# Sliding-window attention and a mixture of experts on one core: sums moved behind the next minimum, one pool of PSUM banks, four stages for seven

## Chip, core and metric

One core of a Trainium2 chip runs the whole kernel. The metric is device time in microseconds, the median of several runs; a profiled execution gives the trace. Engines are called PE (TensorE), DVE (VectorE), ACT (ScalarE), POOL (GpSimd) and SP (the queue that issues most transfers). Names such as L684 are lines of the kernel.

## What is computed

```python
# attention: 8 sequences x 8 heads, 576 positions, head size 64, float32
scores = 1/sqrt(64) * q @ k.T            # heads 0-3: the last 32 positions
                                         # heads 4-7: every 4th of the last 128
attn = softmax(masked scores); x = attn @ v      # x: (4608, 512)
# mixture of 8 experts, each token to one
logits = x @ w_gate; e = argmax(logits); g = softmax(logits)[e]
out = g * (relu(x @ w1[e]) @ w2[e])      # w1: 512 x 1024, w2: 1024 x 512
```

## The kernel before

**Attention.** A sequence has eight units: two types (ty 0 near window, ty 1 every fourth position), two pairs of heads (hl), two halves (g). `front` (L260) makes a unit's scores in PSUM (L270), scales and masks them into `e` on DVE (L282), takes the minimum of each block, `lo` (L292), runs six or eight exponentials on ACT (L295) that leave their sums in `den`, adds 1e-9 (L303) and takes the reciprocal (L305) on DVE, and multiplies on POOL (L306). `weights` (L311) transposes the result on PE (L317) and copies it out as `eT`. `summed` (L324) multiplies by v (L337) and copies out `xT`. `turn` (L216) transposes q and k for the next pair of heads. `attention` (L353) writes, in step i: front of unit i, weights of unit i−2, in every second step the two turns, and summed of unit i−2 (LAG is 2). The copies out of PSUM go by `evac` (L175) to DVE and ACT in turn, so they carry lines 178 and 180.

**Routing.** When a sequence has ended, `route` (L389) transposes its rows (L396), computes logits (L407), the expert of each token and its rank among the tokens of that expert (a DVE chain and two matmuls, L449 and L456), and scatters the rows into a bucket for each expert by six indirect transfers on POOL's queue (L156).

**Experts.** 43 slots of up to 128 tokens of one expert, each 32 matmuls into `ph` (L684), relu, 8 into `py` (L708; each float32 matmul is two records), and a scatter of the result (L717). Which expert a slot has is known only on the chip: `tables` (L494) computes it for a stage of slots in some 25 small DVE operations. A stage's slots are those that must be full after so many sequences. SP loads the tables' values and then the tokens and, if the expert differs from that of the slot two before, 2 MB of w1 and 2 MB of w2 into one of two buffers.

**Order.** All engines issue in written order. The text interleaves three generators: attention, routing and the slots. Each piece has a cost (a scores step 1.2, weights 0.8, a turn 0.7, summed 0.9, a slot's pieces 0.93, 0.88 and 0.5, 14.98 in all). After each attention piece the slots are owed its cost times a rate; a stage's slots may run 14 after its tables were written, and the rate is then what is left, over 42. What is left over when attention and routing have ended runs alone.

**PSUM.** Two tiles of two banks (scores, weights, turned), one bank (xo, routing), two for ph, one for xt and py.

Of the kernel before, what the change touches and what calls it, by code (L numbers as in the profile page):

```python
# [45 lines left out]
def _constants():  # L46
# [23 lines left out]
    }  # L70


    for s, (_, j0, j1) in enumerate(STAGES):
        place = np.append((np.arange(E) - 3 * s) % E, E)
        parts[f"upto{s}"] = np.tile((place[None] <= place[:, None]).reshape(1, -1), (128, 1))
# [15 lines left out]
def kernel(  # L91
# [14 lines left out]
    ctx.enter_context(tc.manual_schedule())  # L106
# [60 lines left out]
    def bank2(name):  # L167
        return big.tile([128, 2, 512], F32, tag="big", name=name)

    def bank(name):  # L170
        return one.tile([128, 512], F32, tag="one", name=name)

    flip = [0]

    def evac(dst, src):  # L175
        flip[0] ^= 1
        if flip[0]:
            nc.vector.tensor_copy(dst, src)  # L178
        else:
            nc.scalar.copy(dst, src)  # L180
# [35 lines left out]
    def turn(b, ty, hl, name):  # L216

        src = t[b, name, ty]  # L220
        dst = pool.tile([128, S], F32, tag=name + "T", name=name + "T", bufs=2)
        ps = bank2("turned")
        if ty == 0:
            for i in range(NT):
                nc.tensor.transpose(  # L225
                    ps[:, i // 3, TT * (i % 3) : TT * (i % 3) + TT],
                    src[:, i, 2 * hl : 2 * hl + 2, :].rearrange("p h d -> p (h d)"),
                    ident[0:TT, 0:TT],
                )
            evac(dst.rearrange("p (a t) -> p a t", a=2), ps[:, :, 0:288])  # L230
        else:
            for h in range(2):
                for m in range(4):
                    nc.tensor.transpose(  # L234
                        ps[:, h, 72 * m : 72 * m + 72],
                        src[:, 2 * hl + h, 128 * m : 128 * m + 128],
                        ident[0:72, 0:72],
                    )
                evac(
                    dst.rearrange("p (h m t a) -> p h a m t", h=2, m=2, a=2)[:, h],  # L240
                    ps[:, h, 0:288].rearrange("p (a m t) -> p a m t", a=2, m=2),
                )
        return dst
# [16 lines left out]
    def front(qT, kT, ty, g):  # L260
# [4 lines left out]
        sc = bank2("scores")  # L265
        for n in range(nb):
            for r in range(2):
                q0, k0, _, _ = bl[r][n]
                rows = slice(DH * r, DH * r + DH)
                nc.tensor.matmul(  # L270
                    sc[0:nq, r, 128 * n : 128 * n + 128],
                    lhsT=qT[rows, q0 : q0 + nq],
                    rhs=kT[rows, k0 : k0 + 128],
                    start=True,
                    stop=True,
                )
# [5 lines left out]
        nc.vector.scalar_tensor_tensor(  # L282
            out=e,
            in0=sc[0:nq, :, 0:w],
            scalar=-SCALE,
            in1=m.unsqueeze(1).broadcast_to([nq, 2, w]),
            op0=OP.mult,
            op1=OP.add,
        )
        ev = e.rearrange("p r (n m) -> p (r n) m", m=128)  # L290
        lo = pool.tile([nq, 2 * nb], F32, tag=f"lo{ty}", name="lo")
        nc.vector.tensor_reduce(out=lo, in_=ev, axis=AX, op=OP.min)  # L292
        den = pool.tile([nq, 2 * nb], F32, tag=f"den{ty}", name="den")
        for n in range(2 * nb):
            nc.scalar.activation(  # L295
                out=ev[:, n],
                in_=ev[:, n],
                func=AF.Exp,
                bias=lo[:, n : n + 1],
                scale=-1.0,  # L300
                accum_out=den[:, n : n + 1],
            )
        nc.vector.tensor_scalar(den, den, 1e-9, None, op0=OP.add)  # L303
        rec = pool.tile([nq, 2 * nb], F32, tag=f"rec{ty}", name="rec")
# [4 lines left out]
        return ev  # L309

    def weights(ev, ty, g):  # L311

        nq, nb = (96, 72)[ty], len(blocks(ty, g)[0])
        tp = bank2("weights")
        for r in range(2):
            for n in range(nb):
                nc.tensor.transpose(  # L317
                    tp[:, r, nq * n : nq * n + nq], ev[:, nb * r + n], ident[0:nq, 0:nq]
                )
        eT = pool.tile([128, 2, 288], F32, tag="eT", name="eT")  # L320
        evac(eT, tp[:, :, 0:288])
        return eT

    def summed(eT, b, xT, ty, hl, g):  # L324
# [20 lines left out]
        if ty == 0:  # L345
            evac(dst, xo[:, 0:288])
        else:
            evac(
# [4 lines left out]
    def attention():  # L353
# [8 lines left out]
        xTs, evs = {}, {}  # L362
        for i in range(len(units) + LAG):
            if i < len(units):
                b, ty, hl, g = units[i]
                evs[i] = front(qT["q"], qT["k"], ty, g)
                yield 1.2, None
            if i >= LAG:
                eT = weights(evs.pop(i - LAG), *[units[i - LAG][n] for n in (1, 3)])
                yield 0.8, None  # L370
# [8 lines left out]
            if i >= LAG:  # L379
# [7 lines left out]
                yield 0.9, (b2, xTs.pop(b2)) if last else None  # L387

    def route(b, xT, bank):  # L389


        rows = []
        for i in range(NT):
# [6 lines left out]
            evac(row[:, 0:DM], ps[0:TT])  # L400
# [85 lines left out]
        for s, (b2, _, _) in enumerate(STAGES):  # L486
            if b2 == b:
                yield
                tables(s, bank)
# [4 lines left out]
    def tables(s, bank):  # L494
# [24 lines left out]
        if last:  # L519
# [18 lines left out]

        ends, end, begin = table("ends", E1, E1), table("end", E1), table("begin", E1)
# [3 lines left out]
            in1=const(f"upto{s}", 1).rearrange("p (a b) -> p a b", b=E1),  # L543
# [114 lines left out]
    def moe():  # L658


        def across(j):
            ps = psy.tile([128, 4, 128], F32, tag="y", name="xt")
# [8 lines left out]
        for j in range(NSLOT):  # L671
# [7 lines left out]
            for fg in range(2):  # L679
                ph = psh.tile([128, 4, 128], F32, tag="h", name="ph")  # L680
# [25 lines left out]
            py = psy.tile([128, 512], F32, tag="y", name="py")  # L706
# [36 lines left out]
    clock = {"moe": 0.0, "all": 0.0, "owed": 0.0, "rate": 0.0, "ready": []}  # L743
    SLOT = 0.5 + 8 * 0.93 + 8 * 0.88

    def run_slots(limit):

        while clock["owed"] > 0:
            now = [r for r in clock["ready"] if r[0] <= clock["all"]]
            upto = max([r[1] for r in now], default=0)  # L750
            if clock["moe"] >= SLOT * upto - 0.01 or clock["moe"] >= limit:
# [7 lines left out]
    def run_routing():  # L759
# [4 lines left out]
        try:  # L764
# [5 lines left out]
            for b2, _, j1 in STAGES:  # L770
                if b2 == b:
                    clock["ready"].append((clock["all"] + 14.0, j1))
                    left = SLOT * j1 - clock["moe"]
                    clock["rate"] = left / 42.0

    for cost, ended in attention():
        clock["all"] += cost
        clock["owed"] += cost * clock["rate"] / 2
        run_slots(1e9)
        if ended:  # L780
            use = bank if ended[0] > 1 else lambda name: psh.tile(
                [128, 512], F32, tag="h", name=name
            )
            routing.append((ended[0], route(*ended, use)))
        run_routing()
        clock["owed"] += cost * clock["rate"] / 2
        run_slots(1e9)
    while routing:
        clock["owed"] = 2.0
        run_slots(1e9)  # L790
# [33 lines left out]
```

## Time and profile before

| | |
|---|---|
| median of 3 runs | 1243.12 us (1242.3 to 1249.36) |
| profiled execution | 1253.76 us, span 1251.5 us |
| PE busy | 998.9 us, 80% of the span; mean granted clock 0.859 |
| DVE, ACT, POOL busy | 376.2 (30%), 305.5 (24%), 202.9 us (16%) |
| transfers | 193 MB, mean 154 GB/s |
| chain that ended last | PE 64%, DVE 15%, ACT 14%, issue 6% |

The shares are means over stretches that differ: attention alone at first, attention with slots, slots alone at the end. A view by stretch (busy time of each engine in windows) and the chain of waits (what released each step of the work that ended last) tell more than the shares. [...]

### The profile page before, as it was taken

The page shows a single profiled execution, that of the slowest core. Times are in us where ns is not written, and L with a number is a line of the kernel's source. Part 1 is how long each engine was busy: PE and PEld are TensorE (multiplying, and loading weights), DVE is VectorE, ACT ScalarE, POOL GpSimd, SP SyncE. Part 2 cuts the span into 40 slices and gives each one's busy share as a digit, 9 for nine tenths or more (in the row PEclk, how much of TensorE's full clock was granted, in tenths as well). Part 3 has the DMA queues.
Part 4 walks back from the last instruction along what each step waited for, and adds up shares of the span by engine and source line. Part 5 has one row for each costly group of instructions (what it writes and reads, how often), then busy time and mean ns, then how long its engine had stood idle before and what let it go on. Part 6 is the DMA issues. An engine that isn't in the chain of part 4 may idle for free.

```text
span 1251.5 us, 18337 instructions
## 1 busy us (share of the span) xinstructions
PE 998.9 (80%) x6922; PEld 762.0 (61%) x6922; DVE 376.2 (30%) x973; ACT 305.5 (24%) x1127; POOL 202.9 (16%) x167
## 2 busy tenths in 40 slices
PE   3546656546768896998789699977979999999996
PEld 2445545445646674666567477755757777777774
DVE  2333333433343334334333533353140110000110
ACT  3333233133123312333233233313100100010100
POOL 1111211211121112112121311122040000000000
PEclk8566556567689968999889999989988999999999
DMA  9022122292066725784338565654567281817910
GB/s 224 1 64 73 38 63 72 76 311 72 6 207 211 250 109 181 229 279 133 82 119 271 182 193 184 202 182 152 170 211 245 103 291 50 286 34 249 320 50 1
DMA packets 137639, 193.23 MB, mean 154 GB/s; under 512 B 68110, under 2 KB 76302, under 8 KB 137424
## 3 DMA queue, kind: packets, MB, share of 16 engines
q1 hardware_dynamic: 129728, 170.98, 42.9%
q0 software_dynamic: 7152, 19.71, 4.5%
q10 hardware_dynamic: 672, 1.37, 0.4%
q8 instruction: 55, 0.90, 0.3%
q14 instruction: 32, 0.26, 0.1%
HBM read 226.60 MB, written 23.11 MB: 200 GB/s over the span
## 4 chain that ended last, share of the span: by engine, by line
PE 64%; DVE 15%; ACT 14%; issue 6%; SPq 1%; DMA 0%; ACTq 0%; POOLq 0%; DVEq 0%
PE ph L684 21%; PE py L708 21%; ACT e L295 12%; PE scores L270 6%; PE xo L337 6%; DVE e L282 5%; DVE lo L292 5%; PE logits L407 4%; PE turned L234 2%; PE xrow L396 2%; PE xt L664 1%; PE turned L225 1%; DVE eT L178 1%; ACT qT L180 1%; ACT kT L180 1%
## 5 line engine op out<-in xcount | busy, mean ns | idle before, releaser
L684 PE MATMUL ph<-xt,w 128*128 128x128 f32 x2752 | 354.0, 284 | 14.5 <-issue 9.5
L684 PEld LDWEIGHTS ph<-xt,w 128*128 128x128 f32 x2752 | 335.8, 198 | 35.4 <-issue 27.4
L708 PE MATMUL py<-w,h 128*128 128x512 f32 x688 | 335.6, 622 | 2.3 <-ACT qT L180 1.8
L295 ACT ACTIVATE e<-e,lo 72x128 f32<-72x128 f32 (+1 forms) x448 | 174.4, 391 | 280.6 <-DVE lo L292 271.5
L306 POOL TENSOR_TENSOR e<-e,rec 96x768 f32<-96x768 f32 (+1 forms) x64 | 107.7, 1683 | 590.0 <-DVE rec L305 292.0
L708 PEld LDWEIGHTS py<-w,h 128*128 128x128 f32 x688 | 124.6, 196 | 115.5 <-issue 109.2
L337 PE MATMUL xo<-eT,v 128*64 128x72 f32 (+1 forms) x896 | 75.2, 297 | 125.4 <-DVE eT L178 60.5
L337 PEld LDWEIGHTS xo<-eT,v 128*64 128x64 f32 x896 | 61.9, 179 | 148.1 <-issue 75.4
L282 DVE SCALAR_TENSOR_TENSOR e<-scores,cst 96x768 f32<-96x768 f32 (+1 forms) x64 | 69.5, 1086 | 179.9 <-PE scores L270 178.6
L666 DVE COPY xt<-xt 128x512 f32<-128x512 f32 x43 | 29.3, 681 | 232.0 <-PE xt L664 218.8
L717 POOL DMA_INDIRECT out_dram<-y,to x43 | 42.6, 990 | 315.1 <-ACT y L712 311.7
L712 ACT ACTIVATE y<-py,x 128x512 f32<-128x512 f32 x43 | 29.4, 683 | 239.8 <-PE py L708 142.2
L270 PE MATMUL scores<-kT,qT 64*72 64x128 f32 (+1 forms) x896 | 82.9, 336 | 4.1 <-DVE qT L178 3.4
L295 ACT ACTIVATION_READ_ACCUMULATOR e<-e,lo 72x1 f32 (+1 forms) x448 | 84.5, 189 | 0.0
L270 PEld LDWEIGHTS scores<-kT,qT 64*72 64x72 f32 (+1 forms) x896 | 65.9, 188 | 29.2 <-issue 20.0
L180 ACT COPY xT<-xo 128x288 f32<-128x288 f32 x57 | 31.7, 555 | 174.6 <-PE xo L337 174.6
L292 DVE TENSOR_REDUCE lo<-e 96x6 f32<-96x768 f32 (+1 forms) x64 | 69.3, 1083 | 2.2
L303 DVE TENSOR_SCALAR den<-den 96x6 f32<-96x6 f32 (+1 forms) x64 | 10.7, 168 | 189.4 <-ACT e L295 182.7
L156 POOL DMA_INDIRECT bucket<-row,idx x48 | 44.6, 929 | 131.9 <-DVE row L478 119.7
L702 DVE TENSOR_SCALAR h<-ph 128x512 f32<-128x512 f32 x43 | 29.3, 682 | 87.3 <-PE ph L684 74.0
L317 PEld LDWEIGHTS weights<-cst,e 72*128 72x128 f32 (+1 forms) x448 | 44.7, 159 | 14.8 <-issue 14.6
L317 PE MATMUL weights<-cst,e 72*128 72x72 f32 (+1 forms) x448 | 50.5, 260 | 0.0
(101 smaller groups left out, 601.3 us busy)
## 6 DMA issues: line engine op xcount, KB each, us to landing
w<-in_moe_w_dram SPq DMA_DIRECT2D x86, 2048.0 KB
x<-bucket SPq DMA_DIRECT2D x43, 257.0 KB
v<-in_v_dram SPq DMA_DIRECT2D x16, 512.0 KB
v<-in_v_dram SPq DMA_DIRECT2D x32, 160.0 KB
q<-in_q_dram SPq DMA_DIRECT2D x32, 144.0 KB
k<-in_k_dram SPq DMA_DIRECT2D x32, 144.0 KB
q<-in_q_dram SPq DMA_DIRECT2D x8, 576.0 KB
k<-in_k_dram SPq DMA_DIRECT2D x8, 576.0 KB
```

What stands on the lines that cost most here:

```text
L156: nc.gpsimd.indirect_dma_start(out=bucket, out_offset=bass.IndirectOffsetOnAxis(ap=idx, axis=0), in_=rows, in_offset=None, bounds_check=NR ...
L180: nc.scalar.copy(dst, src)
L270: nc.tensor.matmul(sc[0:nq, r, 128 * n : 128 * n + 128], lhsT=qT[rows, q0 : q0 + nq], rhs=kT[rows, k0 : k0 + 128], start=True, stop=True,)
L282: nc.vector.scalar_tensor_tensor(out=e, in0=sc[0:nq, :, 0:w], scalar=-SCALE, in1=m.unsqueeze(1).broadcast_to([nq, 2, w]), op0=OP.mult, op1 ...
L292: nc.vector.tensor_reduce(out=lo, in_=ev, axis=AX, op=OP.min)
L295: nc.scalar.activation(out=ev[:, n], in_=ev[:, n], func=AF.Exp, bias=lo[:, n : n + 1], scale=-1.0, accum_out=den[:, n : n + 1],)
L306: nc.gpsimd.tensor_tensor(out=ev, in0=ev, in1=rec.unsqueeze(2).broadcast_to([nq, 2 * nb, 128]), op=OP.mult)
L317: nc.tensor.transpose(tp[:, r, nq * n : nq * n + nq], ev[:, nb * r + n], ident[0:nq, 0:nq])
L337: nc.tensor.matmul(xo[DH * h : DH * h + DH, nq * i : nq * i + nq], lhsT=vv, rhs=eT[:, r, nq * n : nq * n + nq], start=True, stop=True,)
L407: nc.tensor.matmul(lg[:, i], lhsT=xT[:, c, TT * i : TT * i + TT], rhs=wg[:, c], start=c == 0, stop=c == 3,)
L684: nc.tensor.matmul(ph[:, fi], lhsT=w1[:, c, 128 * f : 128 * f + 128], rhs=xt[:, c], start=c == 0, stop=c == 3,)
L708: nc.tensor.matmul(py, lhsT=h[:, f], rhs=w2[:, f], start=f == 0, stop=f == 7)
```

## The change

- `front` ends with the exponentials; a new `norm` (sum, reciprocal, POOL's multiplication) of unit i−1 is written behind `front` of unit i. lo, den and rec get three buffers.
- Only PE and SP keep the written order. The order on DVE, ACT and POOL is chosen when the kernel is built.
- One pool of eight single banks for everything in PSUM; scores, weights and turned tiles become two banks each, and e's first operation, eT and the turned copies become two instructions of half the size.
- Copies of q, k and eT all go to DVE, those of xo to ACT, those of rows to ACT and DVE in turn.
- Stages end after sequences 1, 3, 5 and 7 (before: 1 to 7), with 2, 9, 9 and 23 slots (before: 2, 4, 5, 4, 5, 4, 19). Experts with the most slots come first, an order computed on the chip (`key`, `upto`).
- The interleaving's costs and rates change: a stage's slots may run 16 after its tables, over 36 for each sequence to the next stage and 6.

```diff
-STAGES = [
-    (b, READY[b - 1] if b else 0, READY[b])
-    for b in range(B)
-    if READY[b] > (READY[b - 1] if b else 0)
-]
+TURNS = (1, 3, 5, 7)
+STAGES = [(b, READY[a] if a >= 0 else 0, READY[b]) for a, b in zip((-1, *TURNS), TURNS)]
+    parts["first"] = np.tile(np.append(np.arange(E)[::-1] / E, -1e6), (128, 1))
-    ctx.enter_context(tc.manual_schedule())
+    ctx.enter_context(tc.manual_schedule(engines={mybir.EngineType.PE, mybir.EngineType.SP}))
-    big = ctx.enter_context(tc.tile_pool(name="psbig", bufs=2, space=PSUM))
-    one = ctx.enter_context(tc.tile_pool(name="psone", bufs=1, space=PSUM))
-    psh = ctx.enter_context(tc.tile_pool(name="psh", bufs=2, space=PSUM))
-    psy = ctx.enter_context(tc.tile_pool(name="psy", bufs=1, space=PSUM))
+    psum = ctx.enter_context(tc.tile_pool(name="psum", bufs=8, space=PSUM))
+    def bank(name, *dims):
+        return psum.tile([128, *(dims or (512,))], F32, tag="bank", name=name)
@@ turn
+        for a in range(2):
+            ps = bank("turned")
+            if ty == 0:
...
+                nc.vector.tensor_copy(dst[:, 288 * a : 288 * a + 288], ps[:, 0:288])
@@ front
-        sc = bank2("scores")
+        sc = [bank("scores") for _ in range(2)]
-        nc.vector.scalar_tensor_tensor(out=e, in0=sc[0:nq, :, 0:w], ...)
+        for r in range(2):
+            nc.vector.scalar_tensor_tensor(
+                out=e[:, r], in0=sc[r][0:nq, 0:w], scalar=-SCALE, in1=m, op0=OP.mult, op1=OP.add
+            )
+        return ev, den
+
+    def norm(ev, den, ty, g):
         nc.vector.tensor_scalar(den, den, 1e-9, None, op0=OP.add)
         nc.vector.reciprocal(rec, den)
         nc.gpsimd.tensor_tensor(
             out=ev, in0=ev, in1=rec.unsqueeze(2).broadcast_to([nq, 2 * nb, 128]), op=OP.mult
         )
@@ weights
         for r in range(2):
+            tp = bank("weights")
...
+            nc.vector.tensor_copy(eT[:, r], tp[:, 0:288])
@@ summed
-            evac(dst, xo[:, 0:288])
+            nc.scalar.copy(dst, xo[:, 0:288])
@@ attention
-                evs[i] = front(qT["q"], qT["k"], ty, g)
-                yield 1.2, None
+                evs[i], dens[i] = front(qT["q"], qT["k"], ty, g)
+            if 0 < i <= len(units):
+                norm(evs[i - 1], dens.pop(i - 1), *[units[i - 1][n] for n in (1, 3)])
+            yield 1.0, None
@@ tables
+        key, upto = table("key", E1), table("upto", E1, E1)
+        nc.vector.tensor_tensor(out=key, in0=av, in1=const("first", 1), op=OP.add)
+        nc.vector.tensor_tensor(out=upto, in0=key..., in1=key..., op=OP.is_ge)
@@ run_slots, run_routing
+    ATT, BEHIND = 36.0, 16.0
+            while ready and ready[0][0] <= clock["all"]:
+                _, upto, over = ready.pop(0)
+                clock["upto"] = upto
+                clock["rate"] = (SLOT * upto - clock["moe"]) / over
-                    clock["ready"].append((clock["all"] + 14.0, j1))
-                    left = SLOT * j1 - clock["moe"]
-                    clock["rate"] = left / 42.0
+                    ahead = STAGES[n + 1][0] - b if j1 < NSLOT else 1
+                    ready.append((clock["all"] + BEHIND, j1, ATT * ahead + 6.0))
```

## Rows read from the trace of the kernel before

**Rows 1.** Windows of 50 us: busy us and instructions of each engine, clock, DMA, GB/s.

```profile
150.00:200.00 50.00, 27.47 (x208) 22.75 (x207) 17.65 (x29) 18.82 (x81) 8.61 (x5) 0.53 0.24 55
...
350.00:400.00 50.00, 36.91 (x287) 26.86 (x287) 20.00 (x51) 14.91 (x60) 9.79 (x6) 0.86 0.70 230
...
1150.00:1200.00 50.00, 50.00 (x285) 36.13 (x285) 4.32 (x9) 4.55 (x7) 3.89 (x4) 1.00 0.78 276
```

**Rows 2.** Timeline of PE in the end: start, us, engine, line, operation.

```profile
919.38 4.54 PE L708 MATMUL py<-w,h 128*128 128x512 f32 x10
...
955.38 0.60 PE L664 MATMUL xt<-cst,x 128*128 128x128 f32 x4
...
969.83 0.60 PE L664 MATMUL xt<-cst,x 128*128 128x128 f32 x4
...
1233.51 7.03 PE L708 MATMUL py<-w,h 128*128 128x512 f32 x16
```

**Rows 3.** Chain of waits, 0 to 300 us: start, us, what; starts of sequences among them.

```profile
13.18 1.62 PE scores L270 x12
...
96.66 1.55 PE scores L270 x12
...
136.93 1.94 PE scores L270 x16
138.89 1.23 DVE e L282
140.15 1.23 DVE lo L292
141.46 3.21 ACT e L295 x16
145.14 0.64 DVE eT L178
145.91 1.23 PE xo L337 x12
147.13 1.94 PE scores L270 x16
...
168.24 1.74 PE xo L337 x16
...
190.19 1.55 PE scores L270 x12
191.84 0.96 DVE e L282
```

**Rows 4.** Timeline of DVE at 145 us; in brackets the idle time before, and its releaser.

```profile
144.69 0.21 DVE L303 TENSOR_SCALAR den<-den 72x8 f32<-72x8 f32 x1 [3.33 <-ACT e L295]
...
145.06 0.70 DVE L178 COPY eT<-weights 128x576 f32<-128x576 f32 x1
```

**Rows 5.** Groups of DVE by shape: busy us, mean ns, idle before and releasers.

```profile
L178 DVE COPY eT<-weights 128x576 f32<-128x576 f32 x57 | 41.2, 724 | 8.2 <-PE weights L317 8.2
...
L178 DVE COPY qT<-turned 128x288 f32<-128x288 f32 x16 | 7.3, 456 | 10.0 <-PE turned L234 9.3
```

**Rows 6.** Timeline of PE at the full clock: units 40 and 56, and an xo.

```profile
539.49 0.90 PE L270 MATMUL scores<-kT,qT 64*96 64x128 f32 x12
...
656.04 0.99 PE L337 MATMUL xo<-eT,v 128*64 128x72 f32 x16 [1.54 <-DVE eT L178]
...
775.00 0.90 PE L270 MATMUL scores<-kT,qT 64*96 64x128 f32 x12
```

**Rows 7.** Timeline of POOL at 231 us: a scatter of routing, and the next multiplication.

```profile
231.14 0.95 POOL L156 DMA_INDIRECT bucket<-row,idx  x1 [13.32 <-DVE row L478]
...
238.24 1.90 POOL L306 TENSOR_TENSOR e<-e,rec 72x1024 f32<-72x1024 f32 x1
```

**Rows 8.** Timeline of DVE at 238 us: first operation behind the tables' matmul, the next eT.

```profile
237.76 0.10 DVE L507 COPY cnt<-tot 1x8 f32<-1x8 f32 x1
...
243.13 0.74 DVE L178 COPY eT<-weights 128x576 f32<-128x576 f32 x1
```

More of the change, by code (lines that the diff above doesn't have):

```diff
@@ L386, in attention, with route @@
                 last = (ty2, hl2, g2) == (1, 1, 1)
-                yield 0.9, (b2, xTs.pop(b2)) if last else None
-    def route(b, xT, bank):
+                yield 0.8, (b2, xTs.pop(b2)) if last else None
+    def route(b, xT):
         rows = []
@@ L399, in route @@
             row = pool.tile([TT, ROW], F32, tag="row", name="row", bufs=6)
-            evac(row[:, 0:DM], ps[0:TT])
+            (nc.vector.tensor_copy if i % 2 else nc.scalar.copy)(row[:, 0:DM], ps[0:TT])
             rows.append(row)
@@ L488, in route, with tables @@
                 yield
-                tables(s, bank)
+                tables(s)
     where = {}
-    def tables(s, bank):
+    def tables(s):
         b, j0, j1 = STAGES[s]
@@ L536, in tables @@
         nc.vector.tensor_tensor(out=av[:, 0:E], in0=ns[0:1], in1=us[:, 0:E], op=OP.subtract)
+        key, upto = table("key", E1), table("upto", E1, E1)
+        nc.vector.tensor_tensor(out=key, in0=av, in1=const("first", 1), op=OP.add)
+        nc.vector.tensor_tensor(
+            out=upto,
+            in0=key.unsqueeze(1).broadcast_to([1, E1, E1]),
+            in1=key.unsqueeze(2).broadcast_to([1, E1, E1]),
+            op=OP.is_ge,
+        )
         ends, end, begin = table("ends", E1, E1), table("end", E1), table("begin", E1)
@@ L742, with run_slots @@
     slots, routing = moe(), []
-    clock = {"moe": 0.0, "all": 0.0, "owed": 0.0, "rate": 0.0, "ready": []}
+    clock = {"moe": 0.0, "all": 0.0, "owed": 0.0, "rate": 0.0}
+    ready = []
     SLOT = 0.5 + 8 * 0.93 + 8 * 0.88
-    def run_slots(limit):
+    ATT, BEHIND = 36.0, 16.0
+    def run_slots():
         while clock["owed"] > 0:
-            now = [r for r in clock["ready"] if r[0] <= clock["all"]]
-            upto = max([r[1] for r in now], default=0)
-            if clock["moe"] >= SLOT * upto - 0.01 or clock["moe"] >= limit:
+            while ready and ready[0][0] <= clock["all"]:
+                _, upto, over = ready.pop(0)
+                clock["upto"] = upto
+                clock["rate"] = (SLOT * upto - clock["moe"]) / over
+            if clock["moe"] >= SLOT * clock.get("upto", 0) - 0.01:
                 clock["owed"] = 0.0
@@ L769, in run_routing @@
             fetch()
-            for b2, _, j1 in STAGES:
+            for n, (b2, _, j1) in enumerate(STAGES):
                 if b2 == b:
-                    clock["ready"].append((clock["all"] + 14.0, j1))
-                    left = SLOT * j1 - clock["moe"]
-                    clock["rate"] = left / 42.0
+                    ahead = STAGES[n + 1][0] - b if j1 < NSLOT else 1
+                    ready.append((clock["all"] + BEHIND, j1, ATT * ahead + 6.0))
     for cost, ended in attention():
         clock["all"] += cost
-        clock["owed"] += cost * clock["rate"] / 2
-        run_slots(1e9)
+        clock["owed"] += cost * clock["rate"] / 2 + 1e-6
+        run_slots()
         if ended:
[L781 to L784, printed above, removed]
+            routing.append((ended[0], route(*ended)))
         run_routing()
         clock["owed"] += cost * clock["rate"] / 2
-        run_slots(1e9)
+        run_slots()
     while routing:
         clock["owed"] = 2.0
-        run_slots(1e9)
+        run_slots()
         run_routing()
```

79 lines of the change are left out of this document (26 added, 53 removed).

## The prediction

> **What bounds the kernel now.** I read the busy share by stretch first, then the chain of waits, then TensorE's timeline. The reader sees two kernels in one. From 0 to about 290 us only attention runs: PE is busy 27 of 50 us at a granted clock of 0.53 [rows 1]. In the last 300 us only expert slots run, PE is busy without a gap at full clock [rows 1], and a slot takes 969.83 − 955.38 = 14.45 us [rows 2]. In between both are mixed.
>
> The attention stretch is bound by a ring, not by an engine. The chain of waits for one unit reads: scores 1.94, e 1.23, lo 1.23, eight exponentials 3.21, then eT, xo 1.23, and the next unit's scores, 10.2 us from 136.93 to 147.13 [rows 3]. The exponentials are in the ring for one reason: VectorE takes its instructions in written order, the sum of unit i (L303, L305) is written ahead of the copy eT of unit i−2 (L178), and it waits 3.33 us for ScalarE [rows 4]. The copy needs nothing of unit i, but stands behind it, and PE stands behind the copy. A sequence of eight units without routing takes 96.66 − 13.18 = 83.5 us, so 10.4 us a unit; the next one, with routing, 190.19 − 96.66 = 93.5, so routing adds 10 [rows 3].
>
> **The change part by part.**
>
> *Sums behind the next minimum.* With the sum of unit i−1 behind lo of unit i, its exponentials have had a whole unit to end. The ring becomes e, lo, the sums, eT, xo, scores. Work for a unit of 72 rows, in VectorE's time after the scores: e is cut in two. The nearest row for a cut is the copy, 576 elements in 724 ns against 288 in 456 [rows 5], so one cut costs 2 × 0.456 − 0.724 = 0.19. e 1.23 + 0.19, lo 1.23, sums 0.4 (two of 0.2 [rows 4]), eT in two halves 0.91, hand-offs 0.15: 4.1 us. Then PE's xo 1.74 and scores 1.94 at the low clock [rows 3], 0.99 and 1.2 at the high one (0.90 for twelve matmuls, so 1.2 for sixteen [rows 6]): 7.8 or 6.3 us. A unit of 96 rows (e and lo 0.96, scores 1.55 or 0.90, xo 1.23 or, by the same ratio, 0.7 [rows 3, 6]): 3.5 + 2.8 = 6.3 or 3.5 + 1.6 = 5.1. In every second unit, four copies of q and k (4 × 0.456) run beside xo before the scores: about 0.1 more on the mean at the low clock, 0.4 at the high. Means: 7.1 low, 6.1 high.
>
> Which clock? PE will be busy some 60 to 80% of the time here; the rows give 0.53 at 55% busy and 0.86 at 74% [rows 1]. I take the middle, **6.6 us a unit** for 10.4. [...]
>
> *What now waits in the new place.* The sum of unit i releases GpSimd's multiplication (1.90 us [rows 7]), which the transposes of the weights need two units on. Counted from the scores of unit i+1: e and lo 2.7, sums 0.4, GpSimd 1.9, so 5.0 us, and PE comes for it after one more unit, 6.6. So 1.6 us are left, and none at a pace under 5.0. On GpSimd's queue this multiplication shares with routing's six scatters, 0.92 with 0.3 between them, 7.4 us in a row (from 231.14; the multiplication follows at 238.24 [rows 7]). Behind all six it would come 7.4 − 1.6 = 5.8 us late; before them, not at all. I take 2 us for each of the four routings in the first stretch, 8 in all; in the mixed stretch slots cover it. SP's order is the written one as before; its waits for weight buffers come no earlier, and the loads of q, k and v (a unit pace of 6.6, six units ahead) have some 40 us.
>
> *VectorE and ScalarE no longer in written order.* Where an instruction lands is then a planner's choice; the trace can't show it. Bounds: it puts eT ahead of lo and the sums (a gain of up to 1.6 us in every second unit; 5.5 us a unit), or puts the sums back ahead of eT (a loss; 10.4 as today). I take the written place, since earlier-written work that is ready should go first.
>
> *Evictions that PE waits for move to VectorE.* Today's copies of q and k on ScalarE queue behind exponentials, and PE's second half waits for a bank. VectorE gets about 0.9 us more a unit; its whole work a unit is then about 1.4 + 1.2 + 0.4 + 0.9 + 0.9 = 4.8, plus routing, under 6.6. [...]
>
> *One pool of eight banks.* Two-bank tiles of a pool of two become single banks freed by their own copy. The waits of the transposes of q and k for ScalarE disappear with this. If banks run short, PE waits for an eviction again: between nothing and, per unit, one lo plus the sums, 1.6 to 1.9 us. I take nothing, since e, its longest reader, frees its bank in 1.4 us.
>
> *Four stages for seven.* Each table is a VectorE chain that stands ahead of eT: from 237.76 to 243.13, 5.4 us, and PE waits for the copy behind it [rows 8]. Three are gone: 16 us less; the two additions of key and upto cost 0.4 us a stage by the small operations' 0.2. But slots come later. I followed the planner's own sums by hand for both versions (costs per yield, ready times, rates). Before: 6.4 slots are written when unit 40 starts, 15.3 at unit 56, 21.7 when routing ends (919.38, PE's last table [rows 2]). After: slots 0 and 1 at rate 2 × 14.98/78 = 0.38 from unit 25; 1.1 slots at unit 40; then rate 1.9 up to slot 11, 2.6 from unit 54; 12.3 slots at attention's end, 13.8 when routing ends. So **29.2 slots instead of 21.3 stand alone at the end**, at 14.45 us: 114 us more there.
>
> *Fewer weight loads.* Counting the experts of the reference's own inputs, 30 pairs of loads become 25. They are hidden: a pair is 4.2 MB for a slot of 14.45 us, 290 GB/s; PE had no gap in a stretch that moved 276 [rows 1]. Without that cover the seven loads in eight slots around slots 14 to 21 would cost 0.7 us each, 5 us.
>
> **The sum.** With p a unit's pace in attention that runs nearly alone (units 0 to 39) and N a mixed sequence's time beyond its slots:
> start 13 + 40 p + four routings 40 + two tables 11 + 1.1 slots 16 + GpSimd's lateness 8; then 12.7 slots 183 + 3 N + one table 5 + the last routing's PE work 8; then 29.2 slots 422 + 11 from the last matmul (1233.51 + 7.03 [rows 2]) to the span's end. That is 717 + 40 p + 3 N.
> N today: units 40 to 55 took 775.0 − 539.5 = 235.5 us [rows 6] with 8.8 slots (127 us), so 54 a sequence. With the exponentials out of the ring, PE's waits there shrink; PE's own work is about 33 (8 units of scores 1.0, xo 0.85, and weights and turned somewhat less, by the full-clock rows [rows 6], some 25, and routing's 8). I take N = 47, nearer to today than to the floor, because MoE pieces already filled much.
> 717 + 264 + 141 = 1122 us of span. The profiled execution took 2.3 us more than its span (1253.8), and the median of the runs, 1243.1, is 0.9915 of it: (1122 + 2.3) × 0.9915 = **1115 us**. Between 919.38 and 969.83 there are 50.5 us for 2.6 slots [rows 2]: 13 us of gaps while the last stage's weights come. After, six known slots stand before that stage, so I count none; with them, 13 more.
>
> **The rivals.**
> A, *denser*: the planner lets eT pass lo, and the clock stays full: p = 5.5, N = 42: 717 + 220 + 126 = 1063, 1056 us. For it: eT needs only the weights' transposes, which PE writes right behind the scores. Against: lo is written first and is ready as early.
> B, *VectorE or the banks bind*: q, k, eT copies, routing and minima share one engine, and a late eviction holds a bank: p = 8.5, N = 54: 717 + 340 + 162 = 1219, 1211 us. For it: VectorE's work a unit rises to 4.8, some 6 with routing. Against: it is still under the ring.
> C, *slower*: the change doesn't do what it says, the planned order of VectorE keeps the sums ahead of eT (or eT behind something else that waits for ScalarE), so p stays 10.4 and N 54 (and GpSimd is not late): 709 + 416 + 162 = 1287, 1278 us. The 114 us of slots then bought nothing. It decides from p = (1251 − 717 − 162)/40 = 9.3 upward. Against it: both the written order and readiness put eT first.
>
> **How the numbers follow.** Likeliest (0.50): 1115, its own range 1075 to 1155 (p 6 to 7.2, N 42 to 52). A 0.22, B 0.18, C 0.10. The range takes in most of A (1056, down to 1040) and B up to its middle, 1211; outside lie C (0.10), B's upper half (0.08) and A's lower end. About 1% (12 us) is what a measurement of this kernel can tell from no change. Faster by over 1%: all of the likeliest and A, nearly all of B: 0.87. Within 1%: the ends of B and C, 0.04. Slower: 0.09.
>
> **What would show it.** Right: in the first 200 us scores follow scores in 6 to 7 us; no sum that waits for ScalarE ahead of eT; unit 40 starts near 345 us for 539.5; the stretch of slots alone is 29 slots long at 14.45. Granted clock above 0.7 early. Wrong: xo still waits for a copy that stands behind ScalarE (C); PE waits on banks, or VectorE busy without gaps (B); slots in the tail longer than 14.45 (loads not hidden). A pace over 9.3 would turn the sign.

## The result, and the profile after

| | before | after |
|---|---|---|
| median | 1242.71 us | 1028.85 us (1026.11 to 1031.57) |
| ratio | | 0.827, 95% interval 0.824 to 0.831 |
| profiled execution, its span | 1253.76, 1251.5 us | 1031.57, 1029.5 us |
| PE busy, mean granted clock | 80%, 0.859 | 92%, 0.926 |
| transfers | 193 MB | 172 MB |

The kernel takes 17% less time. The forecast was 1115 us with a range from 1040 to 1211, so the sign was right and the time lies 11 us below the range. The first line below is PE's share on the page of after; then come windows of 50 us, with the columns of [rows 1], in which a clock of 1.00 is the full one.

```profile
PE 944.1 (92%) x6916; PEld 727.1 (71%) x6916; DVE 382.4 (37%) x1114; ACT 278.5 (27%) x1079; POOL 202.5 (20%) x167
```

```profile
50.00:100.00 50.00, 40.46 (x389) 34.68 (x389) 33.20 (x101) 25.00 (x112) 17.27 (x13) 0.74 0.38 87
150.00:200.00 50.00, 36.20 (x337) 30.82 (x333) 29.61 (x76) 23.70 (x105) 11.78 (x7) 0.75 0.89 260
...
350.00:400.00 50.00, 50.00 (x433) 38.30 (x432) 25.34 (x59) 20.85 (x82) 13.11 (x9) 1.00 0.88 249
...
950.00:1000.00 50.00, 50.00 (x295) 37.05 (x294) 5.90 (x11) 4.46 (x7) 2.92 (x3) 1.00 0.38 135
```

From 150 to 200 us PE is busy 36 us for 27 in [rows 1], at a clock of 0.75 for 0.53; from 350 to 400 it has no gap and the full clock, where [rows 1] has 37 us and 0.86. The end was full before and is full now. So the gain lies ahead of the slots alone: in attention by itself and in attention mixed with slots. The starts on PE, to be set against [rows 2, 3, 6]:

```profile
13.18 2.88 PE L251 MATMUL scores<-kT,qT 64*96 64x128 f32 x24
...
118.36 1.60 PE L251 MATMUL scores<-kT,qT 64*96 64x128 f32 x12
...
175.17 1.60 PE L251 MATMUL scores<-kT,qT 64*96 64x128 f32 x12
...
297.85 0.90 PE L251 MATMUL scores<-kT,qT 64*96 64x128 f32 x12
...
465.29 0.90 PE L251 MATMUL scores<-kT,qT 64*96 64x128 f32 x12
...
596.66 0.29 PE L487 MATMUL tot<-counts,cst 96*128 96x8 f32 x2
603.03 0.60 PE L655 MATMUL xt<-cst,x 128*128 128x128 f32 x4
617.48 0.60 PE L655 MATMUL xt<-cst,x 128*128 128x128 f32 x4
...
1011.20 7.03 PE L699 MATMUL py<-w,h 128*128 128x512 f32 x16
```

First a matter of counting, with the first unit as unit 0. The first line holds 24 records, the scores of two units: unit 1 waits for nothing and starts with the 13th, at 14.57 us. The lines behind it are the second units of their sequences, 17, 25, 41 and 57. The same holds in the kernel before: 96.66 is unit 9 and 190.19 unit 17 [rows 3], 539.49 unit 41 and 775.00 unit 57 [rows 6], which the rows and the prediction call starts of sequences and units 40 and 56. So a pace is taken here from unit 1 to unit 9.

Unit 41 starts at 297.9 us (before 539.5, forecast 352 under the name of unit 40). Unit 57 starts at 465.3 (before 775.0). Routing's last table follows at 596.7 (before 919, forecast 689). From there 432.8 us of slots alone remain (forecast 433), one every 617.48 − 603.03 = 14.45 us.

One unit in the first stretch, from the timeline of all engines (the last line from that of PE alone; in brackets the idle time before, and its releaser):

```profile
57.06 1.60 PE L251 MATMUL scores<-kT,qT 64*96 64x128 f32 x12
...
58.77 1.02 DVE L264 SCALAR_TENSOR_TENSOR e<-scores,cst 96x384 f32<-96x384 f32 x2 [1.75 <-PE scores L251]
...
59.70 0.16 DVE L285 TENSOR_SCALAR den<-den 72x8 f32<-72x8 f32 x1
59.77 0.45 DVE L302 COPY eT<-weights 128x288 f32<-128x288 f32 x1
60.14 0.94 DVE L269 TENSOR_REDUCE lo<-e 96x6 f32<-96x768 f32 x1
...
61.00 0.19 DVE L287 RECIPROCAL rec<-den 72x8 f32<-72x8 f32 x1
61.11 0.40 DVE L302 COPY eT<-weights 128x288 f32<-128x288 f32 x1
...
61.57 0.92 PE L318 MATMUL xo<-eT,v 128*64 128x72 f32 x14 [0.95 <-DVE eT L302]
...
62.41 1.60 PE L251 MATMUL scores<-kT,qT 64*96 64x128 f32 x12
```

The sum (L285) doesn't wait for ACT here, unlike [rows 4], and the exponentials are out of the ring. Over the first 300 us DVE does wait at L285 for ACT, 11 times and 11.7 us in all (before 25 times and 72.6 us), but behind the sums the next unit's e or a copy of routing comes then, and not eT. Scores follow scores after 62.41 − 57.06 = 5.35 us here; from unit 1 to unit 9 it is (62.41 − 14.57) / 8 = 5.98 us, for (96.59 − 14.57) / 8 = 10.25 before. And DVE's order is not the one written: den's addition and the first half of eT have passed lo. What is left of the waits, PE's list for the first 300 us (total us, times, longest):

```profile
PE xo L318 <- DVE eT L302: 34.8, 31, 3.2
...
PE xo L318 <- DMA v<-in_v_dram: 4.6, 1, 4.6
...
PE weights L299 <- POOL e L288: 1.4, 1, 1.4
```

The ring still binds at e, half of eT, lo, half of eT, xo; POOL's lateness, priced at 8 us, is 1.4.

### The profile page after: what moved, and what is told of

It reads as the page before. It is cut to its first block, busy times and chain, and to the rows that moved or that the text cites. A ratio compares the mean times of both kernels' runs of the same rounds, so it can differ in the third digit from the quotient of the medians.

```text
span 1029.5 us, 18476 instructions
## 1 busy us (share of the span) xinstructions
PE 944.1 (92%) x6916; PEld 727.1 (71%) x6916; DVE 382.4 (37%) x1114; ACT 278.5 (27%) x1079; POOL 202.5 (20%) x167
## 4 chain that ended last, share of the span: by engine, by line
issue 45%; PE 33%; DVE 11%; DMA 4%; POOL 4%; ACT 3%; SPq 1%; POOLq 0%; DVEq 0%; ACTq 0%
PE py L699 7%; PE scores L251 7%; PE ph L675 6%; PE xo L318 5%; DVE e L264 4%; DVE lo L269 3%; POOL out_dram L708 3%; ACT e L272 3%; PE logits L390 2%; DVE eT L302 2%; PE xrow L379 2%; PE weights L299 2%; DMA v<-in_v_dram 1%; PE turned L207 1%; DMA bucket<-row,idx 1%
## 5 line engine op out<-in xcount | busy, mean ns | idle before, releaser
L675 PE MATMUL ph<-xt,w 128*128 128x128 f32 x2752 | 338.2, 278 | 0.0
L675 PEld LDWEIGHTS ph<-xt,w 128*128 128x128 f32 x2752 | 324.5, 194 | 18.9 <-issue 16.2
L699 PE MATMUL py<-w,h 128*128 128x512 f32 x688 | 318.6, 603 | 0.0
L318 PE MATMUL xo<-eT,v 128*64 128x72 f32 (+1 forms) x896 | 78.9, 277 | 50.4 <-DVE eT L302 38.6
L264 DVE SCALAR_TENSOR_TENSOR e<-scores,cst 72x512 f32<-72x512 f32 (+1 forms) x128 | 73.6, 613 | 90.8 <-PE scores L251 90.8
L302 DVE COPY eT<-weights 128x288 f32<-128x288 f32 x128 | 53.8, 441 | 14.3 <-PE weights L299 14.3
L685 ACT ACTIVATE h<-ph 128x512 f32<-128x512 f32 x43 | 25.6, 595 | 103.8 <-PE ph L675 103.8
```

What stands on the lines that cost most here:

```text
L264: nc.vector.scalar_tensor_tensor(out=e[:, r], in0=sc[r][0:nq, 0:w], scalar=-SCALE, in1=m, op0=OP.mult, op1=OP.add)
L302: nc.vector.tensor_copy(eT[:, r], tp[:, 0:288])
L318: nc.tensor.matmul(xo[DH * h : DH * h + DH, nq * i : nq * i + nq], lhsT=vv, rhs=eT[:, r, nq * n : nq * n + nq], start=True, stop=True,)
L675: nc.tensor.matmul(ph[:, fi], lhsT=w1[:, c, 128 * f : 128 * f + 128], rhs=xt[:, c], start=c == 0, stop=c == 3,)
L699: nc.tensor.matmul(py, lhsT=h[:, f], rhs=w2[:, f], start=f == 0, stop=f == 7)
```

## The experiments

The kernel before ran beside each of them; its median differed between the chips (1242 to 1255 us), so ratios to it are compared. After's is 0.827. Two questions were open: which part made the gain, and why it was larger than the forecast.

**Written order on every engine.** The one line that hands three engines to the planner goes back.

```diff
-    ctx.enter_context(tc.manual_schedule(engines={mybir.EngineType.PE, mybir.EngineType.SP}))
+    ctx.enter_context(tc.manual_schedule())
```

> The changed kernel with all five engines in written order, everything else kept: the sums still stand behind the next unit's minimum. Theory (the ring is broken by the place of the sums, and the planner's order adds the rest): the pace of attention that runs nearly alone is the 6.6 us a unit of my prediction against 6.15 measured in the changed kernel, routing and tables cost some 30 us more, the mixed stretch some 20: 1085 us, range 1050 to 1115. Rival (the planner's order of VectorE, ScalarE and GpSimd is what broke the ring): the pace goes back over 9 us and the time over 1180.

Measured: 1070.3 us, ratio 0.855 (0.853 to 0.858), in the range expected, with a pace of 6.12 us. The written order alone keeps most of the gain; without the planner's order the kernel takes 3.4% longer than after. The waits in the first 300 us, and the first table, from two views of this kernel:

```profile
PE xo L318 <- DVE eT L302: 60.3, 28, 10.0
```

```profile
153.83 0.23 DVE L524 TENSOR_TENSOR upto<-key 1x81 f32<-1x81 f32 x1
...
155.22 2.15 DVE L569 TENSOR_TENSOR ge<-sel,cst 1x18 f32<-1x18 f32 x1
...
159.02 0.80 DVE L302 COPY eT<-weights 128x288 f32<-128x288 f32 x2
...
159.51 1.58 PE L318 MATMUL xo<-eT,v 128*64 128x96 f32 x12 [8.71 <-DVE eT L302]
```

In written order a table stands ahead of eT, and xo waits 8.7 us, as in [rows 8]; in after the table's operations are mixed with e, lo and eT, and xo's longest wait is 3.2. This kernel also has something that after has not, a gap behind the last table:

```profile
623.02 3.73 PE L675 MATMUL ph<-xt,w 128*128 128x128 f32 x32
...
630.55 0.27 PE L675 MATMUL ph<-xt,w 128*128 128x128 f32 x1 [1.73 <-issue]
...
638.31 0.37 PE L675 MATMUL ph<-xt,w 128*128 128x128 f32 x1 [2.42 <-issue]
```

Single matmuls follow each other with pauses of up to 2.4 us for about 13 us. That is the gap which the forecast found before and laid to the weights of the last stage. Here six slots known long before stand between the table and that stage, and the gap is there all the same. It falls into the second half of a slot's ph, whose first half (32 records from 623.02) had run without a pause on the same load of w1; in before it is the same (32 records from 923.76, pauses from 929.69). So that reason is wrong.

**Sums back behind their own front, the planner's order kept.**

```diff
-            if 0 < i <= len(units):
-                norm(evs[i - 1], dens.pop(i - 1), *[units[i - 1][n] for n in (1, 3)])
+                norm(evs[i], dens.pop(i), ty, g)
```

> The changed kernel with sum, reciprocal and multiplication written directly behind the unit's own exponentials again; VectorE, ScalarE and GpSimd are still ordered by the planner. Its VectorE order still has each sum behind the next e and beside the copies eT, so theory: the move of the text is not needed where the planner orders, time within 1% of 1029 us. Rival (the written place matters even so, as a priority): the sums delay eT again, at least 3% slower, 1060 or more.

Measured: 1054.3 us, ratio 0.840 (0.837 to 0.843), 1.5% slower than after by the ratios. Neither side had it: not within 1%, not 3%. Of the 25 us between the profiled executions, 14 are the trickling of ph at the last table, which is back here; the rest lies between units 9 and 41. The pace is (62.02 − 14.36) / 8 = 5.96 us, after's own. So with a planner the written place of the sums hardly matters to the ring.

**Both back.** Written order, and the sums in their old place.

> The changed kernel with the sums in their old place and all engines in written order; banks, evictions, stages and rates as changed. Theory: the ring of exponentials, sums, eT, xo and scores is back, the pace is near 10 us a unit, the mixed sequences cost 54 us beyond their slots, and 29 slots stand alone at the end: 1270 us, range 1220 to 1300, so slower than the kernel before although four other parts of the change are in. Rival (the banks and the evictions off ScalarE carry the gain): 1150 or less.

Measured: 1232.7 us, ratio 0.984 (0.982 to 0.986), in the range expected, 37 us under its middle, but 1.6% faster than before and not slower. The ring is back, in the timeline and in the waits of the first 300 us:

```profile
60.82 0.17 DVE L285 TENSOR_SCALAR den<-den 72x8 f32<-72x8 f32 x1 [3.31 <-ACT e L272]
61.02 0.20 DVE L287 RECIPROCAL rec<-den 72x8 f32<-72x8 f32 x1
61.14 0.77 DVE L302 COPY eT<-weights 128x288 f32<-128x288 f32 x2
61.59 1.58 PE L318 MATMUL xo<-eT,v 128*64 128x96 f32 x12 [4.57 <-DVE eT L302]
```

```profile
PE xo L318 <- DVE eT L302: 99.6, 22, 11.0
```

den waits 3.31 us for ACT, 3.33 in [rows 4]. The pace is 9.79 us. Everything else in the change, banks, cut operations, copies, stages, brings 1.6% together in written order with the sums in their old place; moving the sums there is worth 1232.7 − 1070.3 = 162 us.

**The sums moved alone, in the kernel before.** front is split into front and norm, norm of unit i−1 stands behind front of unit i, and lo, den and rec have three buffers; nothing else changes.

> The kernel before with one part of the change alone: sum, reciprocal and multiplication of unit i-1 written behind the minimum of unit i, three buffers for lo, den and rec. Theory (this is the main part): the first 24 units save about 3 us each, the 40 mixed ones about 1 us each, tail and tables as before: 1130 us, range 1090 to 1160. Rival (evictions behind exponentials on ScalarE and the two-bank tiles hold PE as long as the sums did): 1200 or more.

Measured: 1148.3 us, ratio 0.916 (0.915 to 0.918), as expected. That is 105 us, not 162: the pace is (77.76 − 14.18) / 8 = 7.95 us. PE still waits for the copies of q that ACT makes behind its exponentials (turned waits 22.8 us for qT on ACT in the first 300 us; in before 41.0), and with the copies on DVE, in the first experiment, this wait is not there. So the other parts together are worth 21 us before the sums are moved (1253.6 − 1232.7) and 78 behind it (1148.3 − 1070.3). How much of the 78 belongs to the copies, to the banks or to the stages was not separated in written order.

**Copies to DVE and ACT in turn.** In after, the copies of q, k, eT, xo and rows go by `evac` as before; the cut sizes stay.

```diff
-            nc.vector.tensor_copy(eT[:, r], tp[:, 0:288])
+            evac(eT[:, r], tp[:, 0:288])
```

> The changed kernel with all copies out of PSUM going to VectorE and ScalarE in turn again (q, k, eT, xo, rows); banks, sums, planner's order, stages as changed. Theory (a copy that PE waits for must not stand behind 2.4 to 3.2 us of exponentials): half the eT and q, k copies come late again, about 1 to 1.5 us a unit over 40 units: ratio to the kernel before 0.87, range 0.85 to 0.90, against 0.827. Rival (the planner places them well enough, and ScalarE relieves VectorE): 0.835 or less.

Measured: 1018.2 us, ratio 0.816 (0.812 to 0.819): faster, by 1.2% of before, and my theory fell. The two halves of eT stand on two engines here, and ACT's half is the shorter one (ns shortest/median/longest):

```profile
L164 DVE COPY eT<-weights x64: 411/448/458, 22.2 to 553.3; 128x288 f32<-128x288 f32 x64
...
L164 ACT COPY eT<-weights x64: 375/399/459, 22.6 to 553.3; 128x288 f32<-128x288 f32 x64
```

xo's waits for DVE's eT sink from 34.8 to 11.3 us in the first 300, the pace is 4.66 us. POOL and a load of v come late in their place: weights waits 15.0 us for POOL, xo once 11.0 us for v. Putting all urgent copies on DVE was a loss once the sums were out of ACT's way.

**Seven stages.**

```diff
-TURNS = (1, 3, 5, 7)
+TURNS = tuple(range(1, B))
```

> The changed kernel with seven stages again, one after each sequence from the second on, at the changed interleaving's own rates (over 42 for each); order of experts as changed. My prediction counted 114 us more of slots alone at the end for four stages. Theory (slots moved to the end cost only what they would have filled: PE idle or at the low clock in the first 300 us): seven stages put some 5 slots more there, fill 30 us of gaps, and pay three more tables and weight loads: ratio 0.81, range 0.80 to 0.825. Rival (four stages are the better choice even so: tables ahead of eT, more pairs of weights): 0.835 or more.

Measured: 1011.5 us, ratio 0.813 (0.809 to 0.816), as expected. Unit 41 starts 37 us later than in after and the last table 64 us later, but the end then has 23.0 slots instead of 29.2, 89 us less: 25 us between the two spans, 18 us by the ratios. So four stages are a loss: a slot that is moved to the end costs 14.45 us there, and in the mixed stretch it cost 64 / 6.2 = 10.3, tables and all.

**Four pools of single banks** (four for scores, weights and turned, one for xo and routing, two for ph, one for xt and py).

> The changed kernel with its single banks in four pools: four banks for scores, weights and turned, one for xo and routing, two for ph, one for xt and py; all else as changed. Theory (the banks matter mainly because a single one for xo and routing makes PE wait for the copy before): ratio 0.85, range 0.835 to 0.88. Rival (with evictions on VectorE the pools don't matter): 0.832 or less.

Measured: 1061.4 us, ratio 0.850 (0.846 to 0.855), as expected. One pool is worth 2.3% of before, in the planner's order. The loss lies in the first stretch: unit 41 starts at 332.1 us, 34 later than in after.

**The product with v one unit later.** If the ring left in after is e, lo, eT, xo, then eT needs a unit of its own. weights of unit i−2 stays, summed takes unit i−3.

```diff
-            if i >= LAG:
-                b2, ty2, hl2, g2 = units[i - LAG]
+            if LAG <= i < len(units) + LAG:
+                eTs[i - LAG] = eT
+            if i > LAG:
+                b2, ty2, hl2, g2 = units[i - LAG - 1]
...
-                summed(eT, b2, xTs[b2], ty2, hl2, g2)
+                summed(eTs.pop(i - LAG - 1), b2, xTs[b2], ty2, hl2, g2)
```

> The changed kernel with the sum over v of a unit (its matmuls xo and their copy) written one unit later, three buffers for eT: PE then finds the copy eT ready. Theory (what is left of the ring is PE waiting for eT, 35 us in the first 300, and the low clock that these waits keep): ratio 0.80, range 0.785 to 0.815, pace near 5.3 us a unit, clock above 0.85 in the first 300 us. Rival (VectorE, busy 65% there, binds next): ratio 0.82 or more, with VectorE's waits for PE gone.

Measured: 1006.3 us, ratio 0.808 (0.802 to 0.814), as expected; the pace is 4.87 us. The granted clock was not: 0.79 in the first 300 us, after's 0.78, where over 0.85 was expected; that the waits for eT had kept it low is not shown. PE's waits for those 300 us:

```profile
PE turned L215 <- DMA q<-in_q_dram: 13.6, 1, 13.6
PE weights L299 <- POOL e L288: 11.2, 9, 3.5
...
PE scores L251 <- DVE kT L212: 10.8, 8, 2.9
PE scores L251 <- DVE kT L220: 10.5, 7, 2.8
```

xo's wait for eT is gone. At this pace POOL comes late, as the prediction put it ("none at a pace under 5.0"), the scores wait for the copies of k written just ahead of them, and a load of q is late once.

**The first stage's weights later.** In after one unit waits for v, whose load sits behind 8.4 MB of weights: SP issues four loads of 2048 KB from 156.4 to 164.5 us and that of v from 177.6. The line is from PE's timeline:

```profile
190.61 2.00 PE L318 MATMUL xo<-eT,v 128*64 128x96 f32 x12 [4.60 <-DMA v<-in_v_dram]
```

```diff
-        wanted += [(j, "x", 0, j - 2), (j, "w1", 0, j - 1), (j, "w2", 1, j - 1)]
+        wanted += [(j, "x", 0, j - 2), (j, "w1", 0, j - (j != 1)), (j, "w2", 1, j - (j != 1))]
```

> The changed kernel, with the weights of slot 1 asked for only when slot 0 has used its own; in the changed kernel both pairs, 8.4 MB, are asked for when the first table is ready, and right then PE waits 15 us for v (units 25 to 27, near 190 us). Theory (the first stage's weights stand ahead of q, k and v on SP's queue and the rings): these units fall from 7.5, 10.9 and 15.2 us to about 6, 7 and 12, 8 to 12 us are saved, ratio 0.818, range 0.812 to 0.825. Rival (v is late for another reason, or the second pair collides a little later with the same effect): ratio 0.827 or more.

Measured: 1025.0 us, ratio 0.825 (0.821 to 0.829), at the edge of what was expected, and its interval overlaps after's. The wait, 4.6 us and not the 15 of the expectation, is gone, that unit takes 5.6 us instead of 10.9, and unit 41 starts 7.5 us earlier; the whole kernel's gain can't be told from none.

**Together.** Copies in turn, seven stages and the later product:

> The three variants that gained by themselves, in one kernel: xo one unit later, copies out of PSUM to VectorE and ScalarE in turn, seven stages. Theory (each fills another part of PE's idle time in the first 300 us, but it is the same 70 us of idle time and low clock): the gains add in part, ratio 0.785, range 0.77 to 0.80. Rival (they fill the same gaps): no better than the best of them, 0.805 or more.

Measured: 991.7 us, ratio 0.797 (0.793 to 0.801): the gains add in part, as expected. With the later weights too:

> As the kernel with the three variants, and slot 1's weights asked for only when slot 0 has used its own. Theory: 8 to 15 us less than without, as the stall near 180 us is then the longest of PE: ratio 0.775, range 0.76 to 0.79. Rival (the collision comes back with the next stage's weights): equal within 1%.

Measured: 980.6 us, ratio 0.789 (0.786 to 0.793), 21% under before and 4.6% of after's time under after: the fastest of all, and as expected. The later weights bring 0.8% here, with intervals that just touch. Without them PE waits 12.6 us once for q in this kernel, with them it doesn't. The later product with four stages has such a wait too (13.6 above), seven stages alone have not: it came with the faster pace, not with the stages. The first 300 us in one window, for before, after and this kernel:

```profile
0.00:300.00 300.00, 161.67 (x1224) 136.50 (x1224) 108.89 (x250) 98.86 (x413) 53.66 (x42) 0.62 0.35 97
```

```profile
0.00:300.00 300.00, 231.25 (x2132) 193.90 (x2133) 192.85 (x583) 141.34 (x631) 92.40 (x70) 0.78 0.58 141
```

```profile
0.00:300.00 300.00, 258.84 (x2395) 214.84 (x2396) 188.93 (x558) 163.22 (x701) 95.16 (x73) 0.85 0.71 196
```

PE's busy time goes from 162 by 231 to 259 of 300 us, its clock from 0.62 by 0.78 to 0.85. The same kernel without the copies in turn:

> The kernel with all variants, but the copies out of PSUM placed as in the change (q, k, eT on VectorE, xo on ScalarE) in place of taking turns. Taking turns made attention alone faster (4.8 us a unit for 6.15) and the mixed stretch slower (42 us a sequence beyond its slots for 38.5), and here most of attention is mixed. Theory (the gain of taking turns was the wait for eT, which the later xo removes anyway): equal or better, ratio 0.785, range 0.775 to 0.793. Rival (VectorE binds without ScalarE's help): 0.80 or more.

Measured: 1001.4 us, ratio 0.799 (0.796 to 0.802). The kernel is slower by 1.0% of before, so the expectation fell. But the trace puts most of it in another place than the copies: of 24 us between the two profiled executions, 15 lie behind the last table (358.7 us for 344.1), where the trickling of ph is back:

```profile
656.31 0.37 PE L677 MATMUL ph<-xt,w 128*128 128x128 f32 x1 [2.44 <-issue]
```

Up to unit 41 it loses 3 us and up to the last table another 6. So what the engine of the copies is worth with eT out of the ring is not shown; it is under 10 us in these two executions.

## Why the prediction was right in its mechanism and its span 92 us too long

The span of the profiled executions, by stretches (the forecast calls unit 41 unit 40):

| stretch | forecast | written order (first experiment) | after |
|---|---|---|---|
| to unit 41 | 352 | 314.6 | 297.9 |
| unit 41 to the last table | 337 | 305.6 | 298.8 |
| slots alone, and the end | 433 | 447.6 | 432.8 |
| span | 1122 | 1067.8 | 1029.5 |

**Right.** The ring, and what breaks it: putting the sums back in written order restores it (3.31 us for den), moving them alone breaks it. The forecast's pace of 6.6 us lies near 6.12 in written order and 5.98 in after, before's being 10.25. The slots' pace, their number at the end (29.2) and the hidden loads were right: 432.8 for 433. Rivals B and C didn't happen: DVE is busy 37% of the span (64% of the first 300 us), and no sum stands ahead of eT waiting for ACT.

**What failed: three terms of the sum that were too high, all ahead of the slots alone.** They are the pace (25 us), the constant for routings, tables and POOL (33 us), and the mixed stretch beyond its slots (37 us); the start and the slots make up the small rest.

**40 p, 264 us: measured 239.** The readings behind p had a slip: the 83.5 us from 13.18 to 96.66 are nine units, the first two of them together, so a unit took 10.25 us and a routing added 11.5, not 10.4 and 10. The ring's own sum was too high in VectorE's part. In written order xo starts 0.45 and 0.49 us after the pair of halves of eT does (61.14 and 61.59, 159.02 and 159.51 above): it waits for the first half only. The ring holds some 0.46 us of eT, and the sum counted 0.91. That alone is 0.45 us a unit, nearly all of the 0.48 by which 6.6 exceeds 6.12; what the clock did beside it isn't separated. (The sign given for unit 40, near 345 us, is 7 below the sum's own 352.)

**"I take the written place": priced at nothing, measured 38 us** between the profiled executions (35 by the ratios). The step said that earlier-written work that is ready goes first, and left eT ahead of lo to rival A. The runs show half of A: one half of eT passes lo, den passes both, tables are mixed in instead of standing ahead. From written order to after, 17 us of that lie in the first stretch, 7 in the mixed one, and 15 in the gap behind the last table, whose cause is open. A's own numbers were not met either: 5.5 us a unit for 5.98 measured, at a granted clock of 0.74 (50 to 100 us) and not full.

**The 59 us for routings, tables and POOL: measured 26.** In after the first stretch is 297.9 − 14.6 − 40 × 5.98 − 18 for 1.26 slots = 26 us. In written order the same working, with 6.12, leaves 37, so most of this term's miss has nothing to do with the planner. The starts above tell where it lies. Units 9 to 17, with one routing, take 118.36 − 62.41 = 56.0 us, 8 more than the eight units ahead of them; 12 had been counted with POOL's share, and in written order it is 11.9. Units 17 to 25, with a routing and the first table, take 56.8, so 9 more, where some 17 had been counted: a table costs 1 us here and not 5.4. Units 25 to 41, with two routings, a table and the slots, leave 9 where some 29 had been counted. So the price of a routing [rows 3] was not far off where attention runs alone. It was wrong to add it in full where slots run between: 20 of the 33 us lie there. Whether the slots or the routings run in time that was idle there, the sum can't tell. This term stood in all three rivals (without POOL's 8 us in C), and so the range's low end, 1040, was drawn from A's p and N alone. With the measured 5.98 and 36.3 the prediction's formula still gives 717 + 239 + 109 = 1065 us of span, inside the range; the constant's 33 us then put the time under it.

**N = 47: measured 36.3 a sequence.** Units 41 to 56 take 465.3 − 297.9 = 167.4 us, less 6.56 slots at 14.45. I chose nearer to today's 54 than to the floor of 33 that I had counted from PE's own work; PE being without a gap from 350 to 400 us, the floor was the better measure. Two sequences make 21 us of the mixed stretch's 38. Another 15 lie behind unit 57: 596.7 − 465.3 − 6.0 slots = 45 us for the third sequence, its table and the last routing, for which 47 + 13 had been counted. The last 2 are slots.

**The gap behind the last table: right by luck.** None was counted, since the last stage's weights had been blamed. After indeed has none, but the first experiment, with the same stages and weights, has it.

**Four stages.** In the prediction's sum a slot costs 14.45 us wherever it runs, so the 114 us more at the end are taken off the mixed stretch, and four stages gain the 16 us of three tables. Measured, they lose some 18 us, because a slot in the mixed stretch cost only 10.3.

**The price of a cut, and the clock.** The cut copy and the cut first operation of e, by shape (busy us, mean ns), in after and, of e, before:

```profile
L302 DVE COPY eT<-weights 128x288 f32<-128x288 f32 x128 | 53.8, 441 | 14.3 <-PE weights L299 14.3
L264 DVE SCALAR_TENSOR_TENSOR e<-scores,cst 72x512 f32<-72x512 f32 x64 | 41.0, 678 | 45.4 <-PE scores L251 45.4
```

```profile
L282 DVE SCALAR_TENSOR_TENSOR e<-scores,cst 72x1024 f32<-72x1024 f32 x32 | 39.0, 1220 | 103.0 <-PE scores L270 101.8 <-PE xt L664 1.0
```

By their durations two halves of eT take 2 × 441 − 724 = 158 ns more than the whole [rows 5], two halves of e 2 × 678 − 1220 = 136, where I had taken 190. (Half of the turned copies were cut before already, 128x288 in [rows 5].) But the two durations overlap: 64 halves of e at 678 ns are 43.4 us and keep DVE busy for 41.0, and 32 wholes for 39.0, so a cut of e costs 62 ns of DVE's time.

On the clock, the first stretch got 0.78 at 77% busy, between the 0.53 and 0.86 of [rows 1]. Over the first 300 us it is higher where PE is busier in before, after and the fastest kernel (162, 231 and 259 us busy, 0.62, 0.78 and 0.85), but not in every pair of kernels: with four pools PE was busy 237 us at 0.68. What sets the clock is not shown. The full clock, on which 6.1 us a unit had been worked out, was not reached, though the pace was.

## What to carry to other kernels

Look first for an instruction that waits on another engine and stands ahead of work which doesn't need it: here that one place was worth 162 of 1233 us in written order, and the other parts of the change brought little until it was gone. A cost that was measured where an engine is idle beside it (a routing's 10 us, a table's 5, of which after shows 8 and 1) is no constant: where other work is mixed in, give it a range from near nothing up to that cost, and let the rivals vary it too. In a ring, count of a cut tile only the piece that the next step waits for. An engine whose order a planner makes is an unknown that needs a price, here 38 us that the forecast had at nothing, and the next ring should be looked for at once: shifting the product with v by one unit, copies on two engines, stages as early as possible and the first weights later took another 4.6%.

## What was not expected of the hardware

*VectorE beside GpSimd.* Some small table operations took 1.27 to 2.15 us where POOL's multiplication ran beside them, and 0.15 to 0.17 us elsewhere. In the kernel before (timeline of DVE and POOL):

```profile
593.28 1.91 POOL L306 TENSOR_TENSOR e<-e,rec 72x1024 f32<-72x1024 f32 x1
...
593.84 1.38 DVE L536 TENSOR_TENSOR avail<-ns,used 1x8 f32<-1x8 f32 x1
```

Eight elements take 1.38 us and end with POOL's instruction, at 595.2; another operation of this kind, 1x9, took 0.16 us soon behind it, and a reduction with one input, at 593.36 beside the same multiplication, took 0.44, as in all its seven executions (0.44 to 0.45). The line of `avail` (L536) runs seven times: 1.27 to 1.56 us in the five that run beside this multiplication, each ending 0.02 to 0.03 us behind it, and 0.15 us in the two without it (477.25 and 921.56). In the written-order kernel `ge` above, 2.15 us from 155.22, ends at 157.4, as does a multiplication of POOL; in after the same operation, without a multiplication beside it, took 0.17 us at 148.92:

```profile
155.85 1.48 POOL L288 TENSOR_TENSOR e<-e,rec 96x768 f32<-96x768 f32 x1
```

Both DVE operations have two inputs. What makes them longer is not shown, as no run took the multiplication away.

*The trickling of ph* behind the last table (some 13 us, with pauses that the trace shows no releaser for) appears in before, in both kernels in written order, in the sums moved alone, in the planner's order with the sums back and in the last experiment, and is absent in after and the others. In these traces POOL issues eight blank scatters in that time (in before from 926.4 to 936.4 us, 0.97 to 0.99 us each), but it does so in after too (602.7 to 612.7). Whether the two have to do with each other, and why after escapes, stays open. It is worth some 14 us, so a difference of about 1% between two of these kernels can be this gap alone.
